# Dealing shared PSUM banks by expected release, moving key transposes and preparation in an attention and MLP kernel

## The chip, the cores and the metric

One core of a Trainium2 chip. TensorE multiplies matrices into eight PSUM banks, VectorE and ScalarE read them and work on SBUF, GpSimd works on SBUF, SyncE starts most DMAs; each engine runs its own list of instructions in order and waits on semaphores. The metric is the device time of one execution in microseconds. Before the change it was 1618.06 us, the median of three (1617.95 to 1619.25).

## The reference

An attention over 8 batches of 8 heads, whose keys and values are means of 8 rows each, and two MLPs one after the other on its 4608 tokens of width 512:

```
k_p = k.reshape(B, H, S // 8, 8, D).mean(axis=3)      # v_p in the same way; S 576, D 64
scores = q @ k_p.T / sqrt(D)
attn = exp(scores - max) / (sum + 1e-9)
x = (attn @ v_p), heads side by side                  # 4608 x 512
h = x @ w_in;   x = max(0.01 h, h) @ w_out            # 512 -> 2048 -> 512
h = x @ w_in2;  out = max(h, 0)**2 @ w_out2
```

## The kernel before

Values are float32 throughout. A large product is made of three matmuls on operands split into a high and a low part (`three`, lines 339 to 341).

The work has stages. The attention runs interleaved with the first three token tiles (512 tokens each) of the first MLP: tile 0 up to about 158 us, tile 1 to 315, tile 2 to 450. A unit of a tile is one block f of 128 hidden columns, 16 to a tile: `first(t, f)` makes `h1_t_f` with 12 matmuls, ScalarE and VectorE turn it into `gh` and `gl`, and `second(t, f)` adds it with 12 matmuls into four accumulators `acc1_t_j`. Between two units `advance()` moves the generator `attention()` on by a few steps. From 450 us on three passes of the first MLP follow ("lead" passes, t 0 to 2), whose products are combined from sums of operands in the manner of Strassen, and five passes of the second MLP. Each pass has two halves, `first2` and `second2`; after each of their steps (a hook) the last loop of the file calls `prepare_step()` as long as fewer steps are done than `PACE * hooks`. Those steps make the operands of the second MLP's weights (`wm`, `ops`, `hl` and `s` tiles on VectorE and ScalarE).

The attention takes each batch in five chunks of queries, at tokens 0, 128, 256 (64 wide), 320 and 448. In tile names a batch and the chunk's token stand behind the kind: `s5_448_0` are the scores of the first four heads of batch 5, chunk 448. For each chunk: `stage_a` transposes the queries (`trq`), `stage_b` makes two banks of scores (`s`), VectorE takes the max (`mx`, L625), then either ScalarE makes eight exponentials out of PSUM (L632, up to batch 5) or VectorE subtracts the max out of PSUM and ScalarE makes one exponential (L637, batches 6 and 7); GpSimd normalizes (`p`, L651, L659); `stage_c` transposes the probabilities (`pt` and the remainder `pr`); `stage_d` makes the outputs `o`.

`prepare_k(b)` prepares the keys of a batch: VectorE adds them pairwise, two halves (L405, L411 into `kd`) and a remainder (`rr`); TensorE transposes them (`trk`, L460, and `trr`, L475); ScalarE copies them into `kT`. For batches 3 to 7 this is put ahead of the last chunk (448) of the batch before.

PSUM has four accumulator banks (`ps_a`) and four shared banks (`ps_w`). Every short-lived tile (`h`, `trq`, `trk`, `trr`, `s`, `pt`, `pr`, `o`) comes from `work()` and takes the next shared bank in turn. A tile that takes a bank waits until the reads of its last user are done. Within these waits a scheduler orders each engine's instructions, so the written order is not quite the built one.

Of the kernel before, what the change touches and what calls it, by code (L numbers as in the profile page):

```python
# [8 lines left out]
F32 = mybir.dt.float32  # L9
# [8 lines left out]
P = 128  # L18
POOL = 8
TT = 512  # L20
# [12 lines left out]
def attention_two_mlps(  # L33
# [24 lines left out]
    EARLY = 6  # L58
# [10 lines left out]
    PADS = {0: 88, 3: 48, SHRUNK: 48}  # L69
    DIFF = 384  # L70
    XSTEPS = 3
    PACE = 0.87
    LEAD = 3
    NPASS = len(HALVES) - LEAD
    HMAX = max(HALVES)
# [23 lines left out]
    ps_w = one_stack.enter_context(tc.tile_pool(name="ps_w", bufs=4, space=PSUM))  # L99
# [45 lines left out]
    def temp(name, dt=F32):  # L145
        return tpool.tile([P, TT], dt, tag="t", name=name)

    def work(name, n=TT, early=False):
        if early:
            return ps_a.tile([P, n], F32, tag="acc", name=name)  # L150
        return ps_w.tile([P, n], F32, tag="w", name=name)

    x0 = [dpool.tile([DM, WIDE[t]], F32, name=f"x0_{t}") for t in range(NTILE)]
    x0 += [dpool.tile([DM, HALVES[i // 2]], F32, name=f"x0_{NTILE + i}") for i in range(2 * LEAD)]
# [189 lines left out]
    def attention():  # L344

        with ExitStack() as s:
# [39 lines left out]
            rr = one.tile([NP * RX, 2, D], F32, name="rr")  # L386
# [15 lines left out]
            def pooled(dst, src):  # L402

                for n in (POOL * D // 2, POOL * D // 4):
                    nc.vector.tensor_tensor(  # L405
                        out=src[:, :, 0:n], in0=src[:, :, 0:n], in1=src[:, :, n:2 * n], op=ALU.add
                    )
                last = [src[:, :, i * D:(i + 1) * D] for i in range(2)]
                if len(dst.shape) == 4:
                    last = [one_of.unsqueeze(2).to_broadcast(list(dst.shape)) for one_of in last]  # L410
                nc.vector.tensor_tensor(out=dst, in0=last[0], in1=last[1], op=ALU.add)  # L411
# [44 lines left out]
            def load_v(b):  # L456
                return load_kv(b, v, "v", nc.scalar if b == 0 else None)

            def turned(tr, kd, m):
                nc.tensor.transpose(tr[:, m * P:(m + 1) * P], kd[:, m].rearrange("p i d -> p (i d)"), ident)  # L460
# [20 lines left out]
            def prepare_k(b):  # L481
                kr, kk = KV.pop(("k", b))
                i = b % 2
                kd = ap1.tile([P, NP, 2, D], F32, tag="kd", name=f"kd{b}")
                if b in K_ON_PE:
                    for ps in pooled_pe(f"kp{b}", kk):
                        yield
                    nc.scalar.copy(kd, ps.unsqueeze(2).to_broadcast([P, NP, 2, D]))
                else:
                    for g in range(2):  # L490
                        pooled(kd[:, 2 * g:2 * g + 2], kk[g])
                        if b > 0:
                            yield
                            continue
                        tr = work("trk0") if g == 0 else tr
                        for m in range(2 * g, 2 * g + 2):
                            turned(tr, kd, m)
                        yield
                pooled(rr[:, 1:2], kr)
                if b > 0:  # L500
                    load_v(b)
                    tr = work(f"trk{b}")
                    for m in range(NP):
                        turned(tr, kd, m)
                put_keys(i, tr, slice(0, NP))
                put_rest(i, b)
                yield
# [63 lines left out]
            for b in range(B):  # L571
                at = 0
                for span in range(len(SPANS)):
                    off = 0
                    while off < SPANS[span]:
                        n = min(P, SPANS[span] - off)
# [22 lines left out]
            pr = {}  # L599
# [128 lines left out]
            nch = len(chunks) // B  # L728
# [160 lines left out]
            def outputs():  # L889
                for b, span in ended:  # L890
                    yield from stage_d(b, span)
                    ready[0] = max(ready[0], b + span)
                ended.clear()

            opened, ended = [nch], []
            for i in range(nch + 1, len(chunks)):
                b = chunks[i][0]
                if i == 2 * nch:
                    while opened:
                        yield from finish(opened.pop(0))  # L900
                        yield from outputs()
                    yield from prepare_k(2)
                if i % nch == nch - 1 and 1 < b < B - 1:
                    yield from prepare_k(b + 1)
                if i + 2 < len(chunks):
                    load_q(*chunks[i + 2])
                if i + 1 < len(chunks):
                    stage_a(*chunks[i + 1])
                    yield
                stage_b(*chunks[i])  # L910
                yield
                opened.append(i)
                yield from outputs()
                if i % nch == LAG[min(b, 2)]:
                    yield from prepare_v(b)
                while len(opened) > LAG[min(b, 2)]:
                    yield from finish(opened.pop(0))
                    if b < 2:
                        yield from outputs()
# [61 lines left out]
            nc.sync.dma_start(out=dst[j * P:(j + 1) * P, at:at + step], in_=o[:, skip:skip + step])  # L981

    def second(t, f):
        gh, gl = G.pop((t, f))
        wh, wl = HL.pop(("out", t, f))
        if f == 0:
            A[t] = [ps_a.tile([P, TT], F32, tag="acc", name=f"acc1_{t}_{j}")[:, :WIDE[t]] for j in range(4)]
        acc = A[t]
        for j in range(4):
            js = slice(j * P, (j + 1) * P)  # L990
            three(acc[j], (wh[:, js], wl[:, js]), (gh, gl), f == 0, f == NF - 1)
        if f == NF - 1:
            for j in range(4):
                o = temp(f"o1_{t}_{j}")[:, :WIDE[t]]
                if j % 2 == 0:
                    nc.scalar.copy(o, acc[j])
                else:
                    nc.vector.tensor_copy(o, acc[j])
                store_x1(t, j, o)
# [11 lines left out]
    FIRST2 = []  # L1011
# [377 lines left out]
    prep, preparing, hooks, prepared = None, True, 0, 0  # L1389
# [34 lines left out]
    for i, (t, f) in enumerate(units):  # L1424
        if f == NF - 3 and t + 1 < NTILE:
            while ready[0] * S < min((t + 2) * TT, PLAIN):
                advance()
            put_stores(made)
            load_x(t + 1)
        if f == NF - 1 and t + 1 < NTILE:  # L1430
            split_x(t + 1)

        rate = RATES[min(t, 1)]
        if i + 1 < len(units):
            first(*units[i + 1])
        tick()
        if i + 2 < len(units):
            split_weights("in", *units[i + 2])
        if i + 1 < len(units):
            split_weights("out", *units[i + 1])  # L1440
        while at_work and made < due + rate // 2:
            advance()
        second(t, f)
        tick()
        due += rate
        while at_work and made < due:
            advance()
        if w1 < NF:
            prepare_weights(w1)
            w1 += 1  # L1450
        elif i >= NF - 2:
            held(lambda: next(sums1, None))
            if i % 4 == 0:
                held(lambda: next(sums1, None))
        if i == NF:
            behind(marks[0], 3000)
        if t == NTILE - 1 and f >= NQ - 2 and not at_work:
            if x2pool is None:
                assert not at_work and next(sums1, 1)
                w_early_stack.close()  # L1460
                x2pool = high_stack.enter_context(tc.tile_pool(name="x2", bufs=1, side="right", reuse_waits="tile"))
                dpart = high_stack.enter_context(tc.tile_pool(name="d2", bufs=1, side="right", reuse_waits="tile"))
                ring = high_stack.enter_context(tc.tile_pool(name="ring", bufs=RING, side="right", reuse_waits="tile"))
                load_x2(0)
                tick(9)
                blocks.insert(0, next_block())
            else:
                if xg is None:
                    xg = products_x(0)
                for _ in range(XSTEPS):  # L1470
                    next(xg, None)
# [23 lines left out]
    for t in range(LEAD + NPASS):  # L1495
        lead[0] = t < LEAD
        if t in (LEAD, SHRUNK):
            assert not preparing
            tick(9)
            pass_stack.close()  # L1500
            low_stack.close()
            if t == SHRUNK:
                xspool.append(ctx.enter_context(tc.tile_pool(name="xs", bufs=1, side="right", reuse_waits="tile")))
            gfpool, gopool, tmpool = open_pools(pass_stack, t)
        for half in (first2, second2):
            for _ in half(t):
                tick()
                hooks += 1
                if prepared < PACE * hooks:
                    prepare_step()  # L1510


# [27 lines left out]
```

## Time and profile before

| | |
|---|---|
| timed runs, median (us) | 1618.06 (1617.95 to 1619.25) |
| profiled execution (us) | 1612.93 |
| its span (us) | 1611.2 |
| TensorE busy (us) | 1574.5, 98% |
| VectorE busy (us) | 1355.0, 84% |
| ScalarE busy (us) | 964.0, 60% |
| GpSimd busy (us) | 120.8, 7% |
| mean granted TensorE clock | 0.997 of 2.4 GHz |

The profile is of one execution; the span reaches from its first to its last instruction. TensorE is PE, VectorE DVE, ScalarE ACT, GpSimd POOL. A busy TensorE may still run slowly or be fed short matmuls; an idle one waits, and the trace says for what.

### The profile page before, as it was taken

The page shows a single profiled execution, that of the slowest core. Times are in us where ns is not written, and L with a number is a line of the kernel's source. Part 1 is how long each engine was busy: PE and PEld are TensorE (multiplying, and loading weights), DVE is VectorE, ACT ScalarE, POOL GpSimd, SP SyncE. Part 2 cuts the span into 40 slices and gives each one's busy share as a digit, 9 for nine tenths or more (in the row PEclk, how much of TensorE's full clock was granted, in tenths as well). Part 3 has the DMA queues.
Part 4 walks back from the last instruction along what each step waited for, and adds up shares of the span by engine and source line. Part 5 has one row for each costly group of instructions (what it writes and reads, how often), then busy time and mean ns, then how long its engine had stood idle before and what let it go on. Part 6 is the DMA issues. An engine that isn't in the chain of part 4 may idle for free.

```text
span 1611.2 us, 23281 instructions
## 1 busy us (share of the span) xinstructions
PE 1574.5 (98%) x7960; PEld 1334.9 (83%) x7960; DVE 1355.0 (84%) x1989; ACT 964.0 (60%) x1827; POOL 120.8 (7%) x146
## 2 busy tenths in 40 slices
PE   6999999999999999999999999999999999999999
PEld 5877787778888887887878888888888888998997
DVE  6999688799588897799779778977897799699797
ACT  6786777755666756675676435643563365465454
POOL 3202332233000000000000000000000000000000
PEclk9999999999999999999999999999999999999999
DMA  8765867663558668867785545454555445656655
GB/s 220 229 199 168 242 198 222 204 188 91 174 201 288 231 200 271 296 205 233 270 308 169 190 141 181 148 183 147 168 174 162 159 141 189 229 170 216 196 165 176
DMA packets 211142, 319.79 MB, mean 198 GB/s; under 512 B 54352, under 2 KB 123984, under 8 KB 211024
## 3 DMA queue, kind: packets, MB, share of 16 engines
q1 hardware_dynamic: 207872, 316.60, 60.7%
q10 hardware_dynamic: 3152, 1.70, 0.4%
q8 instruction: 63, 1.03, 0.3%
q14 instruction: 55, 0.45, 0.1%
HBM read 247.46 MB, written 69.21 MB: 197 GB/s over the span
## 4 chain that ended last, share of the span: by engine, by line
PE 70%; DVE 18%; ACT 4%; DMA 4%; issue 3%; SPq 0%; POOL 0%; ACTq 0%; DVEq 0%; POOLq 0%
PE psum L1255 14%; PE psum L341 13%; PE psum L339 13%; PE psum L340 13%; PE psum L1256 7%; DVE ol L1050 3%; ACT x L632 1%; DVE g L1053 1%; PE h L339 1%; PE s L615 1%; PE h L340 1%; PE h L341 1%; PE acc L339 1%; DVE wb_out L1155 1%; DVE xl L1050 1%
## 5 line engine op out<-in xcount | busy, mean ns | idle before, releaser
L1255 PE MATMUL psum<-wb_out,oh 128*128 128x512 f32 x1008 | 349.7, 392 | 0.0
L339 PE MATMUL psum<-xh,wb_in 128*128 128x512 f32 (+1 forms) x896 | 336.6, 376 | 1.8 <-ACT s L1229 1.0
L341 PE MATMUL psum<-xh,wb_in 128*128 128x512 f32 (+1 forms) x896 | 336.4, 376 | 1.3 <-DVE wb_in L1155 1.3
L340 PE MATMUL psum<-xl,wb_in 128*128 128x512 f32 (+1 forms) x896 | 336.4, 375 | 0.0
L1049 ACT CAST oh<-g 128x1024 fp32r<-128x1024 f32 (+1 forms) x224 | 223.1, 997 | 109.4 <-PE psum L1255 54.0
L1256 PE MATMUL psum<-wb_out,ol 128*128 128x256 f32 x1008 | 281.8, 280 | 0.0
L1050 DVE TENSOR_TENSOR ol<-g,oh 128x1024 fp32r<-128x1024 f32 (+1 forms) x224 | 257.1, 1150 | 8.4 <-ACT oh L1049 7.9
L1255 PEld LDWEIGHTS psum<-wb_out,oh 128*128 128x128 f32 x1008 | 189.2, 188 | 41.8
L339 PEld LDWEIGHTS psum<-xh,wb_in 128*128 128x128 f32 x896 | 168.2, 188 | 29.2 <-ACT s L1229 1.7
L341 PEld LDWEIGHTS psum<-xh,wb_in 128*128 128x128 f32 x896 | 168.2, 188 | 27.9 <-DVE wb_in L1155 1.7
L340 PEld LDWEIGHTS psum<-xl,wb_in 128*128 128x128 f32 x896 | 168.2, 188 | 26.0
L1256 PEld LDWEIGHTS psum<-wb_out,ol 128*128 128x128 f32 x1008 | 189.3, 188 | 0.1
L1154 ACT CAST wb_in<-wb_in 128x512 fp32r<-128x512 f32 x128 | 79.4, 621 | 131.4 <-DMA wb_in<-ws_in 74.6
L1053 DVE TENSOR_TENSOR g<-g,g 128x1024 f32<-128x1024 f32 (+1 forms) x128 | 147.0, 1151 | 0.8 <-ACT g L1176 0.8
L1155 DVE TENSOR_TENSOR wb_in<-wb_in 128x512 fp32r<-128x512 f32 x128 | 87.4, 686 | 61.4 <-ACT wb_in L1154 57.6
L341 PE MATMUL psum<-oh,wb_out 128*128 128x512 f32 x336 | 130.8, 390 | 1.0 <-DVE wb_out L1155 1.0
L340 PE MATMUL psum<-ol,wb_out 128*128 128x512 f32 x336 | 131.3, 391 | 0.0
L339 PE MATMUL psum<-oh,wb_out 128*128 128x512 f32 x336 | 130.7, 389 | 0.0
L1154 ACT CAST wb_out<-wb_out 128x512 fp32r<-128x512 f32 x128 | 79.1, 620 | 53.7 <-DMA wb_out<-ws_out 36.0
L1178 DVE SCALAR_TENSOR_TENSOR g<-g 128x1024 f32<-128x1024 f32 (+1 forms) x80 | 89.1, 1115 | 17.1 <-ACT g L1248 16.4
L1155 DVE TENSOR_TENSOR wb_out<-wb_out 128x512 fp32r<-128x512 f32 x128 | 85.7, 683 | 3.2 <-ACT wb_out L1154 3.1
L339 PE MATMUL h<-xh,hl_in 128*128 128x512 f32 x192 | 78.2, 407 | 4.8 <-ACT hl_out L263 2.1
(171 smaller groups left out, 2781.5 us busy)
## 6 DMA issues: line engine op xcount, KB each, us to landing
wb_in<-wd_in SPq DMA_DIRECT2D x96, 512.0 KB, 3.5
wb_out<-wd_out SPq DMA_DIRECT2D x96, 512.0 KB, 3.9
wb_in<-ws_in SPq DMA_DIRECT2D x128, 256.0 KB, 2.7
wb_out<-ws_out SPq DMA_DIRECT2D x128, 256.0 KB, 2.6
xl<-x SPq DMA_DIRECT2D x24, 512.0 KB, 5.1
v<-in_v_dram SPq DMA_DIRECT2D x16, 512.0 KB, 4.4
st_in_out<-in_moe_w_in_dram SPq DMA_DIRECT2D x16, 512.0 KB, 4.1
st_in_out<-in_moe_w_out_dram SPq DMA_DIRECT2D x16, 512.0 KB, 5.2
```

Of the source, the lines that this page charges most:

```text
L339: nc.tensor.matmul(outp, ah, bh, start=first, stop=False, **kw)
L340: nc.tensor.matmul(outp, ah, bl, start=False, stop=False, **kw)
L341: nc.tensor.matmul(outp, al, bh, start=False, stop=last, **kw)
L615: nc.tensor.matmul(sc[:n, 2 * m:2 * m + 2].rearrange("p a x -> p (a x)"), qT[:, 2 * e + m, :n], kT[b % 2][:, 2 * e + m].rearrange("p a x - ...
L1049: nc.scalar.copy(hi, src)
L1050: nc.vector.tensor_tensor(out=lo, in0=src, in1=raw(hi), op=ALU.subtract)
L1053: nc.vector.tensor_tensor(out=out_, in0=a, in1=b, op=ALU.subtract)
L1154: nc.scalar.copy(whole[:, 0], raw(whole[:, 1]))
L1155: nc.vector.tensor_tensor(out=whole[:, 1], in0=raw(whole[:, 1]), in1=raw(whole[:, 0]), op=ALU.subtract)
L1178: nc.vector.scalar_tensor_tensor(out=g, in0=g, scalar=0.0, in1=g, op0=ALU.max, op1=ALU.mult)
L1255: nc.tensor.matmul(outp, ah, b, start=first, stop=False, skip_group_check=True)
L1256: nc.tensor.matmul(outp[:, 1], al, b[:, 0], start=False, stop=last, skip_group_check=True)
```

## The change

There are three parts. `work()` no longer deals the shared banks in turn from the second tile on: it keeps a clock in units of expected TensorE time (`BUSY`), a time at which each bank is expected to come free (its user's `HOLD` after that user's turn), and gives the bank with the earliest one; `second` moves the clock on by the length of a unit. Keys of batches 3 to 7 have their sums put ahead of the last chunk of the batch before, as until now, but their transposes behind its scores and behind the outputs; the remainder's sum and the loads of the values move up behind the second half's sum. `PACE` becomes a pair: 1.12 steps a hook in the first 28 hooks of a pass, 0.62 in the others.

```
+    HOLD = {"h": 2.2, "trq": 1.6, "trk": 1.8, "trr": 1.5, "pt": 2.2, "pr": 1.8, "o": 1.4}
+    BUSY = {"h": 2.7, "trq": 0.45, "trk": 0.5, "trr": 0.2, "pt": 0.45, "pr": 0.15, "o": 0.5, "s": 0.5}
+    free, clock, chosen = [0.0] * 4, [0.0], [False, 0]
     def work(name, n=TT, early=False):
...
-        return ps_w.tile([P, n], F32, tag="w", name=name)
+        kind = name.split("_")[0].rstrip("0123456789")
+        if chosen[0]:
+            i = min(range(4), key=lambda j: (free[j], (j - chosen[1]) % 4))
+            clock[0] = max(clock[0], free[i]) + BUSY[kind]
+            hold = HOLD.get(kind)
+            if hold is None:
+                b, e = int(name.split("_")[0][1:]), int(name.split("_")[2])
+                hold = (2.4, 2.8)[e] if b >= EARLY else (3.7, 6.0)[e]
+            free[i] = clock[0] + hold
+        else:
+            i = chosen[1]
+        chosen[1] = (i + 1) % 4
+        return ps_w.tile([P, TT], F32, tag=f"w{i}", name=name, bufs=1)[:, :n]
...
                         if b > 0:
+                            if b > 1 and g == 1:
+                                pooled(rr[:, 1:2], kr)
+                                load_v(b)
                             yield
...
                 if i % nch == nch - 1 and 1 < b < B - 1:
-                    yield from prepare_k(b + 1)
+                    keys = prepare_k(b + 1)
+                    for _ in range(2):
+                        next(keys)
+                        yield
...
                 yield from outputs()
+                yield from keys
...
     def second(t, f):
+        clock[0] += BUSY["h"]
...
         rate = RATES[min(t, 1)]
+        chosen[0] = t > 0
...
-    PACE = 0.87
+    PACE = (1.12, 0.62)
...
-                if prepared < PACE * hooks:
+                whole, part = divmod(hooks, 2 * len(FIRST2))
+                more = max(0, part - len(FIRST2))
+                if prepared < sum(PACE) * len(FIRST2) * whole + PACE[0] * (part - more) + PACE[1] * more:
                     prepare_step()
```

On VectorE, before the change, at the hand-over from batch 6 to 7 (`k7_0` and `kd7` are key sums, `pt1_6` and `pt_r` subtractions that read banks of transposed probabilities, `mx6_320` and `x6_320` read score banks):

```order
L405 TENSOR_TENSOR k7_0_4267<-k7_0_4267 128x2x256
L676 TENSOR_TENSOR pt1_6_4276<-pt6_0_4283,pt0_6_4275 128x4x128
L973 TENSOR_TENSOR gl1_2_3_4257<-g1_2_3_4254,gh1_2_3_4256 128x512
L689 TENSOR_TENSOR pt_r_189<-pr6_0_4290,pt_r_189 32x2x128
L405 TENSOR_TENSOR k7_0_4267<-k7_0_4267 128x2x128
L288 TENSOR_TENSOR s1_in6_4238<-s1_in6_4238,w1_6_827 128x256
L411 TENSOR_TENSOR kd7_4351<-k7_0_4267 128x256
L289 TENSOR_TENSOR s1_in6_4238<-w1_6_827,s1_in6_4238 128x256
L264 TENSOR_TENSOR hl_in_2_5_4376<-w1_5_743,hl_in_2_5_4376 128x512
L625 TENSOR_REDUCE mx6_320_0_4325<-s6_320_0_4319 128x4
L625 TENSOR_REDUCE mx6_320_1_4327<-s6_320_1_4322 128x4
L637 TENSOR_TENSOR x6_320_4316<-s6_320_0_4319,mx6_320_0_4325 128x288
```

And of the changed kernel at the same place (its lines are numbered 16 to 25 higher there):

```order
L697 TENSOR_TENSOR pt1_6_4276<-pt6_0_4283,pt0_6_4275 128x4x128
L998 TENSOR_TENSOR gl1_2_3_4257<-g1_2_3_4254,gh1_2_3_4256 128x512
L304 TENSOR_TENSOR s1_in6_4238<-s1_in6_4238,w1_6_827 128x256
L710 TENSOR_TENSOR pt_r_189<-pr6_0_4290,pt_r_189 32x2x128
L305 TENSOR_TENSOR s1_in6_4238<-w1_6_827,s1_in6_4238 128x256
L280 TENSOR_TENSOR hl_in_2_5_4376<-w1_5_743,hl_in_2_5_4376 128x512
L421 TENSOR_TENSOR k7_0_4267<-k7_0_4267 128x2x256
L646 TENSOR_REDUCE mx6_320_0_4325<-s6_320_0_4319 128x4
L646 TENSOR_REDUCE mx6_320_1_4327<-s6_320_1_4322 128x4
L658 TENSOR_TENSOR x6_320_4316<-s6_320_0_4319,mx6_320_0_4325 128x288
```

The first key sum moved behind six operations, and the other two of that half behind the score subtractions.

On TensorE, before, at the hand-over from batch 5 to 6 (`trk6` transposes keys, `s5_448` are the last chunk's scores):

```order
L686 MATMUL pr5_128_3791<-ident_149,p5_128_3506 96x128 x2
L339 MATMUL acc1_1_0_1959<-gh1_1_15_3722,hl_out_1_15_3732 128x512
L340 MATMUL acc1_1_0_1959<-gl1_1_15_3723,hl_out_1_15_3732 128x512
L460 MATMUL trk6_3815<-ident_149,kd6_3796 128x128 x2
L341 MATMUL acc1_1_0_1959<-gh1_1_15_3722,hl_out_1_15_3732 128x512
L339 MATMUL acc1_1_1_1960<-gh1_1_15_3722,hl_out_1_15_3732 128x512
```

And of the changed kernel there:

```order
L707 MATMUL pr5_128_3791<-ident_149,p5_128_3506 96x128 x2
L636 MATMUL s5_448_0_3827<-kT1_181,qT5_448_3742 128x144 x2
L476 MATMUL trk6_3897<-ident_149,kd6_3796 128x128 x2
L355 MATMUL acc1_1_0_1959<-gh1_1_15_3722,hl_out_1_15_3732 128x512
L356 MATMUL acc1_1_0_1959<-gl1_1_15_3723,hl_out_1_15_3732 128x512
L357 MATMUL acc1_1_0_1959<-gh1_1_15_3722,hl_out_1_15_3732 128x512
```

Two acc matmuls moved behind the first keys, and the scores of chunk 448, which stood behind the first `h` of the next tile, stand ahead of the keys.

On TensorE, before, in batch 3, from the scores of chunk 320 on:

```order
L615 MATMUL s3_320_1_2619<-kT1_181,qT3_320_2401 128x144 x2
L671 MATMUL pt3_128_2640<-ident_149,p3_128_2378 128x128 x4
L686 MATMUL pr3_128_2647<-ident_149,p3_128_2378 96x128 x2
L339 MATMUL acc1_1_0_1959<-gh1_1_6_2566,hl_out_1_6_2576 128x512
L340 MATMUL acc1_1_0_1959<-gl1_1_6_2567,hl_out_1_6_2576 128x512
L341 MATMUL acc1_1_0_1959<-gh1_1_6_2566,hl_out_1_6_2576 128x512
L339 MATMUL acc1_1_1_1960<-gh1_1_6_2566,hl_out_1_6_2576 128x512
L340 MATMUL acc1_1_1_1960<-gl1_1_6_2567,hl_out_1_6_2576 128x512
L341 MATMUL acc1_1_1_1960<-gh1_1_6_2566,hl_out_1_6_2576 128x512
L339 MATMUL h1_1_7_2661<-xh1_1_0_1773,hl_in_1_7_2573 128x512
```

And of the changed kernel there:

```order
L636 MATMUL s3_320_1_2619<-kT1_181,qT3_320_2401 128x144 x2
L692 MATMUL pt3_128_2640<-ident_149,p3_128_2378 128x128 x4
L707 MATMUL pr3_128_2647<-ident_149,p3_128_2378 96x128 x2
L355 MATMUL acc1_1_0_1959<-gh1_1_6_2566,hl_out_1_6_2576 128x512
L356 MATMUL acc1_1_0_1959<-gl1_1_6_2567,hl_out_1_6_2576 128x512
L357 MATMUL acc1_1_0_1959<-gh1_1_6_2566,hl_out_1_6_2576 128x512
L355 MATMUL acc1_1_1_1960<-gh1_1_6_2566,hl_out_1_6_2576 128x512
L636 MATMUL s3_448_0_2713<-kT1_181,qT3_448_2598 128x144 x2
L356 MATMUL acc1_1_1_1960<-gl1_1_6_2567,hl_out_1_6_2576 128x512
```

After the chunk's transposed probabilities there were six acc matmuls and then an `h`; now there are four, and then the scores of the last chunk.

## Rows read from the trace of the kernel before

**Rows 1.** First part of the page: busy time of each engine, share, instructions.

```profile
PE 1574.5 (98%) x7960; PEld 1334.9 (83%) x7960; DVE 1355.0 (84%) x1989; ACT 964.0 (60%) x1827; POOL 120.8 (7%) x146
```

**Rows 2.** Stretches: length, then busy time (instructions) by engine, granted clock, DMA.

```profile
50.00:100.00 50.00, 47.86 (x249) 39.80 (x248) 49.05 (x76) 38.33 (x87) 10.40 (x9) 0.97 0.67 210
150.00:300.00 150.00, 146.24 (x811) 119.66 (x810) 115.80 (x252) 115.90 (x452) 47.58 (x59) 1.00 0.71 217
300.00:450.00 150.00, 142.24 (x757) 116.28 (x755) 122.92 (x260) 90.01 (x212) 38.12 (x43) 1.00 0.51 154
450.40:526.60 76.20, 76.20 (x336) 63.12 (x337) 63.09 (x88) 50.39 (x67) 0.00 (x0) 1.00 0.78 269
526.60:603.40 76.80, 76.80 (x338) 62.84 (x337) 72.09 (x100) 50.27 (x73) 0.00 (x0) 1.00 0.63 208
```

**Rows 3.** TensorE's waits from 450 to 920: us in total, times, longest.

```profile
PE psum L341 <- DVE wb_in L1155: 1.3, 1, 1.3
PE psum L339 <- ACT s L1229: 1.0, 1, 1.0
PE psum L341 <- DVE wb_out L1155: 1.0, 1, 1.0
```

**Rows 4.** VectorE's timeline at 348: start, length, operation, [idle before, releaser].

```profile
348.25 1.82 DVE L405 TENSOR_TENSOR k<-k 128x512 f32<-128x512 f32 x1 [1.71 <-DMA k<-in_k_dram]
...
354.55 0.81 DVE L637 TENSOR_TENSOR x<-s,mx 128x288 f32<-128x288 f32 x2
```

**Rows 5.** TensorE's timeline, 351 to 361.

```profile
351.86 0.63 PE L671 MATMUL pt<-ident,p 128*128 128x128 f32 x4 [0.38 <-DVE pt_r L689]
...
355.14 0.47 PE L339 MATMUL h<-xh,hl_in 128*128 128x512 f32 x1 [1.74 <-DVE x L637]
...
360.75 0.44 PE L460 MATMUL trk<-ident,kd 128*128 128x128 f32 x2 [0.79 <-DVE kd L411]
```

**Rows 6.** TensorE's timeline, 85 to 88.

```profile
85.92 0.47 PE L339 MATMUL h<-xh,hl_in 128*128 128x512 f32 x1 [2.14 <-ACT hl_out L263]
...
86.47 0.39 PE L341 MATMUL h<-xh,hl_in 128*128 128x512 f32 x1
86.69 0.40 PE L339 MATMUL h<-xh,hl_in 128*128 128x512 f32 x1
...
87.54 0.63 PE L339 MATMUL h<-xh,hl_in 128*128 128x512 f32 x1
87.97 0.63 PE L340 MATMUL h<-xl,hl_in 128*128 128x512 f32 x1
```

**Rows 7.** TensorE's timeline, 310 to 323.

```profile
310.37 0.41 PE L460 MATMUL trk<-ident,kd 128*128 128x128 f32 x2 [1.50 <-DVE rs L645]
...
314.26 0.24 PE L475 MATMUL trr<-ident,rr 64*128 64x64 f32 x1 [0.90 <-DVE rr L411]
...
322.84 0.50 PE L339 MATMUL acc<-gh,hl_out 128*128 128x512 f32 x1 [1.39 <-ACT o L996]
```

**Rows 8.** VectorE's timeline, 307 to 311.

```profile
307.86 1.96 DVE L405 TENSOR_TENSOR k<-k 128x512 f32<-128x512 f32 x4
...
310.26 0.64 DVE L676 TENSOR_TENSOR pt<-pt,pt 128x512 fp32r<-128x512 f32 x1
```

**Rows 9.** TensorE's waits from 100 to 450: us in total, times, longest.

```profile
PE o L339 <- ACT x L632: 1.4, 3, 0.5
...
PE pt L671 <- POOL p L651: 1.2, 1, 1.2
PE s L615 <- ACT x L632: 1.0, 2, 0.5
```

**Rows 10.** TensorE's timeline, 220 to 225.

```profile
220.51 1.14 PE L615 MATMUL s<-kT,qT 128*128 128x144 f32 x8
...
224.41 0.51 PE L339 MATMUL h<-xh,hl_in 128*128 128x512 f32 x1 [0.71 <-ACT x L632]
```

**Rows 11.** VectorE's timeline at 607, ahead of the operand `wb_in`.

```profile
606.67 0.68 DVE L245 CUSTOM_DVE_ANT_0 ops_out<-ops_out,wm_out 128x1024 uint16<-128x1024 uint16 x1
```

More of the change, by code (lines that the diff above doesn't have):

```diff
@@ L498, in prepare_k @@
                         yield
-                pooled(rr[:, 1:2], kr)
+                if b < 2:
+                    pooled(rr[:, 1:2], kr)
+                if b == 1:
+                    load_v(b)
                 if b > 0:
-                    load_v(b)
                     tr = work(f"trk{b}")
@@ L893, in outputs @@
                 ended.clear()
-            opened, ended = [nch], []
+            opened, ended, keys = [nch], [], iter(())
             for i in range(nch + 1, len(chunks)):
```

## The prediction

> **What bounds the kernel now.** I read the page's busy times first, then busy time by stretch, then TensorE's waits, then the timelines around the longest of them. TensorE is busy 98% of a span of 1611.2 us [rows 1], so a change of order can only give back idle time, and where that lies decides everything. By stretch [rows 2] TensorE is idle 3.8 us in 150 to 300 us (150 less 146.24) and 7.8 us in 300 to 450 (150 less 142.24). In the first Strassen-like pass of layer 1, from 450.4 on, both half passes show TensorE busy throughout. The new dealing of banks starts with the second tile, at about 158 us, and the new order of the keys a little later, so those two parts have 3.8 + 7.8 = 11.6 us to win at most. The preparation by half passes has the waits of the three lead passes, 1.3 + 1.0 + 1.0 = 3.3 us [rows 3].
>
> **Keys of the last batch (hand-over from batch 6 to 7).** Here the trace shows a cause and its effect. VectorE stands 1.71 us at 348.25 before `k<-k`, the first key sum, because the DMA of the keys has not landed, and then spends 1.82 us in it [rows 4]. The sums of the probabilities, the max of the scores and their subtraction stand behind it. TensorE therefore waits .38 at 351.86 for a bank (pt_r), 1.74 at 355.14 for the subtraction at 354.55 that frees a score bank, and .79 at 360.75 for the second half of the key means [rows 4, 5]. A matmul that restarts the engine is .08 longer than its neighbours (0.47 at 85.92 against 0.39 at 86.47) [rows 6], so these are 2.91 + 3 x .08, about 3.2 us. In the built order the first key sum stands behind six operations that it delayed before, and the second one behind the score subtraction of chunk 320; both transposes of the keys now stand after eight acc matmuls. The DMA has landed by 348.25 [rows 4]; the sum's new place comes after that, so VectorE doesn't stop. The sum still stands ahead of the max: 1.82 us instead of 1.71 + 1.82, and the six operations that pass it now fill the stop, so scores are subtracted about 1.7 us earlier (354.55 less 1.71), as much as the wait of 1.74. The transposes come 2 us of acc matmuls later, which covers the .79. I take -3.2. Bounds: -3.2 (nothing is left) and -.5 (only the pt_r wait of .38 and its restart go).
>
> **Keys of batch 6 (hand-over from 5 to 6).** TensorE waits 1.50 at 310.37 for the first key means, .90 at 314.26 for the rest keys, 1.39 at 322.84 for an accumulator that ScalarE copies out behind eight exponentials [rows 7]: 3.79 + 3 x .08 = 4.0. Now the scores of chunk 448 stand ahead of the transposes, and wait for the bank that the probabilities' subtraction frees. That subtraction (310.26) ran behind the four key sums (1.96 from 307.86) [rows 8]; it now stands ahead, so it ends between 308.9 (310.26 - 1.96 + .64) and 309.5, as its ScalarE half may lie between exponentials. TensorE comes there two acc matmuls earlier than to the old wait: 310.37 - 1.50 - 2 x .23 = 308.4. So a new wait of .5 to 1.1; I take 1.1. The later key sums keep a wait of about .7 of the .90, and the accumulator's wait about half of its 1.39, since those exponentials start earlier. Left: 1.1 + .7 + .7 = 2.5, a gain of 1.5. Bounds: -4.0 (all goes) and +1.0 (the new wait is added and only the transposes' 1.50 shrinks by half).
>
> **Banks dealt by expected release, batches 2 to 5.** The waits there name the exponentials: .71 for `h`, 1.4 for `o`, 1.0 for `s` [rows 9, 10]. A score bank is held from 220.51 until the exponentials have read it at 224.41, 3.9 us [rows 10], while TensorE comes back for it 3.2 us later (3.9 - .71). Any dealing must wait for such a bank if all four are held. In the new order of batch 3, scores `s3_448_0` take the place of `h1_1_7` behind the bank of `s3_320_0`, with four acc matmuls between instead of six; two matmuls of .23 fewer make the wait .46 longer. Batch 4 shows the same shift by .43 at its hand-over. Against that, I let .4 of the `o` and `s` waits go, where an output gets a bank that a transpose held. Sum +.46 + .43 - .4, about +.5. Bounds: -3.1 (all three kinds go) and +4.4 (the wait of 1.17, which is .71 + .46, at four more places is 4.7, less .3 regained).
>
> **First tile.** It deals in turn still, but the values of batch 2 load a step earlier, and their sums on VectorE and their mask on GpSimd now stand ahead of the last probabilities of batch 1, for which TensorE waits 1.2 [rows 9]. Between -1.2 (it goes) and +1.2 (it doubles); two h matmuls (.46) now stand ahead of that wait, and some .8 of vector sums too: +.3.
>
> **Preparation by half passes.** The pace rises by .25 a hook in the first 28 hooks and falls by .25 in the others: 7 steps a pass moved forward, on paper. VectorE is busy 63.09 of 76.20 us in a first half and 72.09 of 76.80 in a second [rows 2]; seven steps of the 1.2 us that the largest takes would fit into the first half (71.5). But the order built from it has nearly as many preparation instructions per half as before (42, 15, 42, 18, 44, 7 against 42, 14, 42, 18, 41, 11 on VectorE): the queues were already ahead of the pace. Of the three waits [rows 3] the one for `wb_in` has one `ops_out` instruction more ahead of it (pitch .6) [rows 11] and the others the same work. Take +.3; bounds -3.3 (all three go) and +1.2 (two such steps). What hides the rest of these moves is the second half's slack of 4.7 us; if it were gone, each moved step would cost its 1.2.
>
> **Sum.** -3.2 - 1.5 + .5 + .3 + .3 = -3.6 us. Against the profiled execution: it took 1612.93, the span 1611.2 and 1.7 around it; 1609.3 after. That run lies 5.13 us below the median of the timed ones, 1618.06, and I put the same difference on it: 1614.5 us.
>
> **TensorE's clock.** After the wait of 2.14 us at 85.92 the h matmuls of 87.54 and later start .43 apart, against .22 at 86.47, and the granted clock of 50 to 100 is .97 [rows 2, 6]: the engine fell to the lower of its two levels, 1.2 GHz for 2.4. After the 1.74 us at 355.14 [rows 5] the granted clock of the stretch stays at 1.00 [rows 2]. So a longer wait can be paid a second time, twelve matmuls x .20 = 2.4 us, as it was paid there from 87.5 to 90.1. The Trainium skill, "TensorE: Matmul & The Clock Gate", section "Part 1: The HAM clock gate (the "warmup" mystery)", says that the throttled clock is the default and activity releases it. By that rule, new waits of the change could cost more than they last; the trace agrees at 85.92 and shows no fall after the wait at 355.14. It speaks against a change that puts scores ahead of other work at a full set of banks. The sum would be 1614.5 without and 1616.9 with one such fall.
>
> **Rivals.**
> A. The waits only move: whoever comes next at a held bank waits as long. For: the releases are set by ScalarE's exponentials and VectorE's chain, and neither gets shorter; TensorE arrives earlier wherever a wait was removed. Against: the stop at 348.25 is a stop for a DMA, and it goes. The time is then 1618 (1616 to 1620).
> B. The dealing works as its table says. Of the 11.6 us, all but about 1.5 go: 10 us less, 1608. For: four banks in turn make a free bank wait behind a held one. Against: [rows 10] show a hold of 3.9 us, which exceeds the work at hand whoever gets the bank.
> C. Slower: at the five hand-overs the scores of the last chunk are put ahead of the key transposes and reach a bank still under the previous chunk's exponentials. Price: 3.9 us of hold less the work between, 1.17 us each, 5 x 1.17 = 5.9, less the .71 that it replaces: +5.2, 1623, if the two late hand-overs gain nothing besides. It decides as soon as the hold exceeds the four acc matmuls and two transposes between. For: the hold of 3.9 us [rows 10]. Against: in batches 6 and 7 the scores are freed by one subtraction, not by four exponentials. If the clock falls once as at 85.92, it is 1625.6; that has .03 of its chance.
> D. The change doesn't do what it says: the pace moves nothing, as counted above. That alone costs nothing and is in the forecast.
>
> **How the numbers follow.** Forecast (1611 to 1616) .42; A .26; B .16; C .16. A measurement of this kernel tells about .2%, 3.2 us, from no change. So faster means below 1614.8, same 1614.8 to 1621.3. The forecast's case is split, .34 faster and .08 same; A is all same; B all faster; C slower, but for .01 that ends under the bound. Faster .50, same .35, slower .15. The likeliest case's own range is 1611 to 1616; for 8 in 10 I reach to B's 1608 and, as A is likelier than C, to 1620.5: 1607.5 to 1620.5. The bounds summed, -14.8 to +7.3 from 1618.06, are wider, but their ends need every term to fall the same way.
>
> **What would show it.** Around 348 VectorE no longer stops before `k<-k`, and the wait of 1.74 at the h matmul that follows is under .5: right for the first term. A wait of `s` for a bank at the hand-over to batch 6 of about 1.1, and together under 2.5 there, for the second. Waits of `s3_448_0` and `s4_448_0` of 1.2 for the third. If TensorE's idle time from 150 to 300 falls below 2 us, B was right; if it rises above 7, C. The lead passes should keep three waits of about 1 us. It is wrong if idle time from 300 to 450 stays near 7.8, or if a new stop with a lower granted clock appears.

## The result, and the profile after

The changed kernel takes 1624.57 us, the median of five (1623.49 to 1626.43), against 1617.95 for the kernel before, timed with it (five runs, 1613.13 to 1619.25). The ratio is 1.0058, 95% interval 1.0041 to 1.0074: slower by 0.4 to 0.7%, where 1614.5 and faster was forecast, and above the range's upper end of 1620.5. The two medians alone differ by 6.6 us, the lower end of that interval, since the five runs of before fall into two groups, three at 1618 to 1619 and two at 1613. The profiled execution took 1625.12 us, its span 1623.4; that is 12.2 us above the profiled span of before.

First part of the page of after, which answers to [rows 1]:

```profile
PE 1581.7 (97%) x7960; PEld 1337.3 (82%) x7960; DVE 1361.2 (84%) x1989; ACT 967.5 (60%) x1827; POOL 118.2 (7%) x146
```

TensorE is busy 7.2 us longer with as many instructions. So more than half of the difference between the two profiles is no idle time at all. Where it lies shows when stretches are cut at the same matmuls in both traces, not at the same times. Here are first `h` of tile 0 to first `h` of tile 1, from there to the last `h` of tile 2, and from there to the end of the lead passes, before and then after (columns as in [rows 2]):

```profile
39.43:158.26 118.83, 114.31 (x568) 93.59 (x569) 114.59 (x183) 90.73 (x201) 20.80 (x15) 0.99 0.61 195
158.26:441.21 282.95, 271.90 (x1488) 222.53 (x1487) 223.09 (x481) 195.25 (x641) 84.89 (x100) 1.00 0.63 191
441.21:915.27 474.06, 469.93 (x2066) 386.58 (x2064) 414.57 (x573) 310.53 (x418) 0.00 (x0) 1.00 0.71 239
```

```profile
42.10:163.22 121.12, 115.20 (x571) 93.29 (x570) 114.96 (x184) 91.53 (x201) 20.25 (x15) 0.99 0.64 196
163.22:450.80 287.58, 274.86 (x1489) 222.47 (x1488) 228.07 (x479) 196.08 (x641) 82.74 (x100) 1.00 0.61 186
450.80:927.32 476.52, 471.23 (x2065) 386.68 (x2064) 415.23 (x573) 312.06 (x418) 0.00 (x0) 1.00 0.72 237
```

| stretch | before | after | more |
|---|---|---|---|
| up to the first h | 39.43 | 42.10 | 2.67 |
| first tile | 118.83 | 121.12 | 2.29 |
| second and third tile | 282.95 | 287.58 | 4.63 |
| lead passes | 474.06 | 476.52 | 2.46 |
| all that follows | | | 0.1 |

The first 2.67 us are not the change's: below, executions of kernels alike up to there reach that matmul at 39.4 to 39.7 us or at 42.1 to 42.7. In the second and third tile the busy time alone grows by 2.96 (274.86 less 271.90) and the idle time by 1.67. So waits make the smaller part of the loss there.

**The waits that answer to the forecast.** VectorE of after at the last key hand-over, for [rows 4]:

```profile
354.30 0.82 DVE L579 SCALAR_TENSOR_TENSOR vM<-vd,side_of,vM 128x256 fp32r<-128x256 f32 x2
356.45 0.69 DVE L697 TENSOR_TENSOR pt<-pt,pt 128x512 fp32r<-128x512 f32 x1 [1.33 <-ACT pt L694]
...
360.58 0.69 DVE L421 TENSOR_TENSOR k<-k 128x512 f32<-128x512 f32 x1
...
362.04 0.81 DVE L658 TENSOR_TENSOR x<-s,mx 128x288 f32<-128x288 f32 x2
```

ScalarE at the same place:

```profile
355.34 0.60 ACT L994 ACTIVATE g<-h 128x512 f32<-128x512 f32 x1 [1.58 <-PE h L357]
355.84 0.58 ACT L694 CAST pt<-pt 128x512 fp32r<-128x512 f32 x1
```

and TensorE, for the wait of 1.74 in [rows 5]:

```profile
362.63 0.47 PE L355 MATMUL h<-xh,hl_in 128*128 128x512 f32 x1 [1.09 <-DVE x L658]
```

The stop for the DMA is gone, as forecast; in its place VectorE stops 1.33 us before the subtraction `pt`, for ScalarE's cast `pt`, which stands behind an activation of `h` that ends 355.94. Part of that second stop had been hidden behind the first: before, VectorE stood still from 346.54 (348.25 less 1.71), and the same cast ended only at 347.43.

```profile
346.85 0.58 ACT L673 CAST pt<-pt 128x512 fp32r<-128x512 f32 x1
```

The `h` matmul still waits 1.09. At the hand-over to batch 6 the six waits of TensorE in the trace of after, the two of the scores (.64 and .27) among them, sum to 3.2 us; the forecast had 2.5.

TensorE in batch 3, for [rows 10]:

```profile
225.05 1.22 PE L636 MATMUL s<-kT,qT 128*128 128x144 f32 x8
...
227.46 0.40 PE L355 MATMUL acc<-gh,hl_out 128*128 128x512 f32 x1
230.20 0.76 PE L636 MATMUL s<-kT,qT 128*128 128x144 f32 x4 [2.35 <-ACT x L653]
230.70 0.49 PE L356 MATMUL acc<-gl,hl_out 128*128 128x512 f32 x1
231.03 0.39 PE L357 MATMUL acc<-gh,hl_out 128*128 128x512 f32 x1
231.26 0.40 PE L355 MATMUL acc<-gh,hl_out 128*128 128x512 f32 x1
```

The scores of chunk 448 reach the bank of the scores before them and wait 2.35 us; [rows 10] had .71 at that bank for an `h`. The bank is held 5.2 us (225.05 to 230.20) and not 3.9, because the max comes late from VectorE and the exponentials begin 3.8 us after the first of those scores, before 2.5:

```profile
228.83 0.32 ACT L653 ACTIVATE x<-s,mx 128x72 f32<-128x72 f32 x1 [2.96 <-DVE mx L646]
```

Mark 230.70 to 231.03 too: after a change of operands the second matmul starts .33 behind the first, the next ones .23. TensorE of after changes between kinds of tile some 290 times in the second and third tile, before 262 times, and 29 x .1 would make the 2.96 us of busy time. But the number of changes alone does not make it. The dealing alone has 317 changes and as much more busy time (274.93), and the four tags in turn have 280 and no more busy time than before (271.39):

```profile
161.05:447.76 286.71, 274.93 (x1488) 222.18 (x1487) 224.94 (x478) 195.37 (x641) 85.56 (x100) 1.00 0.62 186
164.26:446.10 281.84, 271.39 (x1489) 222.89 (x1487) 222.51 (x478) 194.65 (x641) 84.15 (x100) 1.00 0.63 189
```

What makes the busy time longer stays open.

TensorE's waits of after in the lead passes, for [rows 3]:

```profile
PE psum L356 <- DVE ol L1076: 1.7, 2, 0.9
PE psum L355 <- ACT s L1255: 1.3, 1, 1.3
PE psum L355 <- ACT oh L1075: 1.2, 1, 1.2
```

Waits for conversions of the pass, `ol` twice and `oh`, stand where two for weights (`wb`) were.

### The profile page after: what moved, and what is told of

It reads as the page before. It is cut to its first block, busy times and chain, and to the rows that moved or that the text cites. A ratio compares the mean times of both kernels' runs of the same rounds, so it can differ in the third digit from the quotient of the medians.

```text
span 1623.4 us, 23240 instructions
## 1 busy us (share of the span) xinstructions
PE 1581.7 (97%) x7960; PEld 1337.3 (82%) x7960; DVE 1361.2 (84%) x1989; ACT 967.5 (60%) x1827; POOL 118.2 (7%) x146
## 4 chain that ended last, share of the span: by engine, by line
PE 70%; DVE 17%; ACT 4%; issue 4%; DMA 3%; POOL 0%; SPq 0%; ACTq 0%; DVEq 0%; POOLq 0%
PE psum L1281 14%; PE psum L356 13%; PE psum L357 13%; PE psum L355 13%; PE psum L1282 7%; DVE ol L1076 2%; ACT x L653 2%; PE h L355 1%; PE h L356 1%; PE h L357 1%; DVE g L1079 1%; PE s L636 1%; DVE mx L646 1%; PE acc L355 1%; PE acc L356 1%
```

## The experiments

Each ratio is to the kernel before on the same chip, with its 95% interval; in the experiments the median of before was 1614.9 to 1615.4. The third column is the ratio's excess times 1615.

| kernel | ratio | more, us | tiles on a bank not the first free |
|---|---|---|---|
| before | 1 | | 3 of 236 |
| after | 1.0058 [1.0041, 1.0074] | 9.4 | 95 of 241 |
| dealing alone | 1.0055 [1.0043, 1.0067] | 8.9 | 95 of 239 |
| keys alone | 1.0004 [0.9996, 1.0013] | 0.6 | 6 of 238 |
| pace alone | 1.0018 [1.0008, 1.0029] | 2.9 | |
| four tags, in turn | 1.0006 [0.9997, 1.0014] | 1.0 | 40 of 241 |
| dealing, measured table | 1.0038 [1.0024, 1.0051] | 6.1 | 51 of 241 |
| keys and pace | 1.0021 [1.0011, 1.0030] | 3.4 | 6 of 239 |
| keys all late | 1.0015 [1.0006, 1.0024] | 2.4 | 7 of 239 |
| pace turned round | 1.0000 [0.9991, 1.0009] | 0.0 | |
| banks as the pool gave them | 1.0015 [1.0005, 1.0026] | 2.4 | 17 of 239 |
| dealing from tile 2 on | 1.0027 [1.0015, 1.0038] | 4.4 | 46 of 241 |

The last column is read from one trace each: of the tiles that take a shared bank between 158 and 455 us, those whose bank's last read ended over .3 us later than that of another bank at that point of the dealing (good to about 2). The count does not set the price by itself: the four tags in turn have 40 such tiles and cost 1.0, the banks as the pool gave them 17 and 2.4.

**The dealing alone.** The edits to `work()`, `second` and `chosen` of the change, the rest as before.

```
...
-        return ps_w.tile([P, n], F32, tag="w", name=name)
+        return ps_w.tile([P, TT], F32, tag=f"w{i}", name=name, bufs=1)[:, :n]
...
```

> Only the dealing of the shared banks (with its four one-bank tags); keys and pace as before. Theory 1 (the dealing costs): 5 to 7 us slower than before, about 2 of it in the first tile (40 to 158 us), the rest between 158 and 315. Theory 2 (the key order costs): within 2 us of before. Theory 3 (the extra 12 us of the two profiled runs is mostly the start-up): within 2 us, and any difference lies before 45 us.

1624.02 us, 1.0055: theory 1. The dealing is nearly all of the loss.

**Keys alone.** The edits to `prepare_k` and the loop over chunks.

```
-                    yield from prepare_k(b + 1)
+                    keys = prepare_k(b + 1)
...
```

> Only the keys' transposes behind the scores, banks in turn and pace as before. Theory 1: 1 to 3 us faster, since the stop of VectorE before the keys of batch 7 goes and the first tile is not touched. Theory 2: 4 to 6 us slower, with new waits of the last chunks' scores at the five hand-overs, 1.2 us each.

1616.16 us, 1.0004: neither; the gain is not there, nor is the loss. TensorE at the hand-over to batch 6 in this kernel:

```profile
319.76 0.27 PE L475 MATMUL trr<-ident,rr 64*128 64x64 f32 x1 [1.46 <-ACT x L637]
321.02 0.43 PE L676 MATMUL pt<-ident,p 64*128 64x64 f32 x4 [0.98 <-issue]
...
323.76 0.80 PE L339 MATMUL acc<-gh,hl_out 128*128 128x512 f32 x1 [1.93 <-ACT o L1005]
...
326.20 0.63 PE L341 MATMUL acc<-gh,hl_out 128*128 128x512 f32 x1
326.62 0.63 PE L339 MATMUL acc<-gh,hl_out 128*128 128x512 f32 x1
```

Three waits of 1.46, .98 and 1.93 us follow within 6 us, and up to 328.33 the matmuls start some .43 apart; the granted clock of this stretch is .77:

```profile
315.00:330.00 15.00, 10.53 (x42) 8.14 (x41) 11.41 (x26) 6.85 (x28) 5.71 (x5) 0.77 0.69 210
```

New waits took the old ones' place, and the lower of the clock's two levels cost some 10 x .20 more. And VectorE's first key sum stands where it stood, with its stop:

```profile
352.72 0.80 DVE L405 TENSOR_TENSOR k<-k 128x512 f32<-128x512 f32 x1 [1.37 <-DMA k<-in_k_dram]
```

**Pace alone.**

```
-    PACE = 0.87
+    PACE = (1.12, 0.62)
...
```

> Only the pace of the preparation, 1.12 and 0.62 a hook instead of 0.87. Theory 1: 1.5 to 3 us slower, all of it in the lead passes (450 to 915 us): the waits of oh and ol operands that the changed kernel shows at 545, 613 and 755 come from it. Theory 2, as predicted: within 0.5 us, the three waits of about 1 us stay and no new one comes.

1617.55 us, 1.0018: theory 1, and its profile is 3.1 us longer in the lead passes. SyncE's queue of this kernel in the second pass, and what follows on ScalarE and TensorE:

```profile
720.54 0.33 SPq L215 DMA_DIRECT2D st_out_out<-in_moe_w_out_dram  x1
...
721.40 0.42 SPq L215 DMA_DIRECT2D st_out_out<-in_moe_w_out_dram  x1
722.51 3.04 SPq L1143 DMA_DIRECT2D wb_out<-ws_out  x2
```

```profile
729.67 0.62 ACT L1154 CAST wb_out<-wb_out 128x512 fp32r<-128x512 f32 x1 [3.55 <-DMA wb_out<-ws_out]
730.19 1.04 ACT L1049 CAST oh<-g 128x1024 fp32r<-128x1024 f32 x1
```

```profile
731.29 0.50 PE L339 MATMUL psum<-oh,wb_out 128*128 128x512 f32 x1 [0.65 <-ACT oh L1049]
732.55 0.50 PE L340 MATMUL psum<-ol,wb_out 128*128 128x512 f32 x1 [0.76 <-DVE ol L1050]
```

Before, SyncE issued these two loads of `st_out_out` nearly 11 us later:

```profile
731.29 0.33 SPq L215 DMA_DIRECT2D st_out_out<-in_moe_w_out_dram  x1
...
732.15 0.42 SPq L215 DMA_DIRECT2D st_out_out<-in_moe_w_out_dram  x1
```

Moved forward, they stand ahead of the weights `wb_out` on their queue. ScalarE stops 3.55 us for those weights with the conversion `oh` queued behind, and TensorE waits for `oh` and for `ol`, .65 and .76. This is one place; in the whole of its lead passes the waits for `oh` and `ol` sum to 4.2 us, where before had 3.3 for weights and `s`. The term was counted on VectorE and ScalarE, where little moves; the loads that a step issues were left out.

**Four tags, in turn.** The dealing alone with `chosen` never set:

```
-        chosen[0] = t > 0
+        chosen[0] = False
```

> The four shared banks as four tags of one bank each, but dealt strictly in turn throughout; keys and pace as before. If the way in which the banks are declared, not the choice among them, moves the first tile: 1.5 to 3 us slower than before, the difference made between 40 and 158 us, and the dealing kernel adds 3 to 4 to it. If the choice alone costs: within 0.5 us of before.

1615.86 us, 1.0006: the choice costs, some 8 us of the 9. But the first tile is 2.8 us longer in the trace, as in every kernel with the four tags (2.3 to 3.4), and the same wait is new there; TensorE's waits of after and of this kernel in the first tile:

```profile
PE h L355 <- ACT g L994: 1.6, 1, 1.6
```

```profile
PE h L355 <- ACT g L985: 1.8, 1, 1.8
```

In its profile the second and third tile give 1.1 of that back. And with the keys in their old order VectorE's first key sum of batch 7 stands behind the subtraction `pt` here, without a stop for the DMA:

```profile
357.74 0.69 DVE L421 TENSOR_TENSOR k<-k 128x512 f32<-128x512 f32 x1
```

So the four tags move that sum, not the new order of the keys.

**The table mended.** The dealing alone with holds from the trace of before.

```
-    HOLD = {"h": 2.2, "trq": 1.6, "trk": 1.8, "trr": 1.5, "pt": 2.2, "pr": 1.8, "o": 1.4}
+    HOLD = {"h": 0.9, "trq": 1.0, "trk": 1.75, "trr": 0.9, "pt": 2.1, "pr": 2.75, "o": 1.65}
...
-                hold = (2.4, 2.8)[e] if b >= EARLY else (3.7, 6.0)[e]
+                hold = (2.45, 2.35)[e] if b >= EARLY else (2.75, 2.95)[e]
```

> The dealing alone (keys and pace as before), with its table set to the holds that the trace of before shows (first write to last read, less BUSY: h 0.9, trq 1.0, trk 1.75, trr 0.9, pt 2.1, pr 2.75, o 1.65, scores 2.75 and 2.95, in the last two batches 2.45 and 2.35). Theory A, the table is wrong: at most 2 us slower than before, as the four tags in turn, and under 40 of some 240 tiles get a bank that is not the first to come free. Theory B, a bank fixed in written order cannot follow the order that is built: still 5 us or more slower, 60 or more of such tiles.

1621.63 us, 1.0038. Closer to theory B, with the count of wrong banks between the two: from 95 to 51. The second score bank of a chunk was down with 6.0 us and its median in batches 2 to 5 is 3.8 from first write to last read. The better table gives back some 3 us (the intervals overlap a little), not 8.

**Keys and pace.** The change without the dealing.

> The changed kernel with the pool's own dealing of the shared banks: keys and pace changed. Theory A and B alike (the dealing costs 8 us, the pace 3, the keys nothing): 2 to 5 us slower than before. If the parts cost by working together instead: within 1 us of before, or 7 us and more slower.

1617.86 us, 1.0021, as the sum of the parts, 0.6 + 2.9. With the dealing's 8.9 the parts sum to 12.4, above the 9.4 (6.6 to 12.0) of the whole; so the parts may not be quite independent.

**Keys all late.** The whole preparation behind the scores and outputs.

```
-                if i % nch == nch - 1 and 1 < b < B - 1:
-                    yield from prepare_k(b + 1)
...
                 yield from outputs()
+                if i % nch == nch - 1 and 1 < b < B - 1:
+                    yield from prepare_k(b + 1)
```

> Banks and pace as before; the whole preparation of the keys of batches 3 to 7, sums as well as transposes, written behind the last chunk's scores and the outputs. If VectorE's stop before the first key sum causes the wait of 1.74 us at the h matmul of 355, as predicted: the stop and that wait go, and the time is 1 to 3 us below before, unless the later transposes delay the next batch. If another chain sets that wait: no change there, and the time within 1 us, or 2 to 4 us slower where the first scores of the next batch wait for the keys.

1616.95 us, 1.0015, slower. VectorE's stop for the DMA goes, and the wait at that `h` with it, but a stop of 1.23 us for ScalarE's `pt` appears, and TensorE waits 1.10 for the keys and .74 for a subtraction of scores:

```profile
352.97 0.69 DVE L676 TENSOR_TENSOR pt<-pt,pt 128x512 fp32r<-128x512 f32 x1 [1.23 <-ACT pt L673]
```

```profile
365.80 0.44 PE L460 MATMUL trk<-ident,kd 128*128 128x128 f32 x2 [1.10 <-DVE kd L411]
...
367.85 0.43 PE L671 MATMUL pt<-ident,p 64*128 64x64 f32 x4 [0.74 <-DVE x L637]
```

**Pace turned round.**

```
-    PACE = 0.87
+    PACE = (0.62, 1.12)
...
```

> Only the pace, turned round: 0.62 steps a hook in the first half of a pass and 1.12 in the second. If steps moved forward cost because their loads and ScalarE conversions come in front of operands of the pass: 1 to 3 us faster than before, with fewer waits in the lead passes. If any move away from an even pace costs: 2 to 5 us slower, with new waits in the second halves, where VectorE is busy 72 of 77 us already.

1615.03 us, 1.0000: neither. In time, held-back steps cost nothing and win nothing. But its profiled execution was the slowest of its eleven, and its lead passes there take 477.5 us, 3.4 more than before's and as long as with the pace of the change (477.1). So the traces do not show where the 2.9 us of that pace lie.

**Banks as the pool gave them.** The four tags, with the kernel before's own bank for each tile name.

```
+        if name in AS_BUILT:
+            i = AS_BUILT[name]
...
```

> The four one-bank tags, each tile by its name in the very bank that the pool gave it in the kernel before; keys and pace as before. If the choice of the bank is what costs: within 2 us of before, and about as many tiles as there (3 of 236) get a bank that is not the first to come free. If a bank fixed at the time of writing costs by itself, whichever it is: 5 us or more slower, with the first tile 2 to 3 us longer.

1618.05 us, 1.0015: between the two, nearer to the first. The first tile is again 3.1 us longer; second and third tile take 281.3 us, no more than before. A list of banks does not bring the order back: 22 of the 321 shared tiles are still first written behind one that the code takes later.

**Dealing from the third tile on.**

```
-        chosen[0] = t > 0
+        chosen[0] = t > 1
```

> The dealing by expected release from the third tile on only (t over 1) instead of the second, in turn before; keys and pace as before. If it costs wherever it deals: between the four tags in turn (+0.9) and the dealing alone (+9), about 4 to 6 us slower, the second tile (158 to 315 us) as long as with the tags in turn. If the second tile's four exponential-bound batches make the cost: under 2 us slower.

1618.93 us, 1.0027: it costs wherever it deals, about half (4.4 of 8.9) with one tile instead of two. Of these runs none beats the kernel before.

## Why the prediction was wrong

**The step that failed is the term on the banks, +.5 us, and with it what is said above of the kernel before: that it deals its banks in turn.** It does not. The first shared tiles of before lie on banks 0 3 2 1 3 0 2 1 0 2 3 1 2 0 3 2, and later all but 3 of 236 lie on one that came free first. Its shared tiles are first written in the very order in which the code takes them, and the pool of one tag gives each a bank that is free at that point of the built order. The change fixes the bank where a tile is written in the code, before the times are known, and with four tags the order itself comes apart as well: in turn 32 of the 321 shared tiles are first written behind one that the code takes later, in the changed kernel 51, in the kernel before none. I read "in turn" off the source. So rival B's premise was false, and the term was priced as a few waits that lengthen. One place shows what a bank fixed beforehand costs: at 403.31 an `h` of after waits for a bank whose last reader is VectorE's `pt`, while the bank of `trq` had been read at 401.37.

```profile
403.31 0.50 PE L355 MATMUL h<-xh,hl_in 128*128 128x512 f32 x1 [1.79 <-DVE pt L697]
```

```profile
402.57 0.68 DVE L697 TENSOR_TENSOR pt<-pt,pt 128x512 fp32r<-128x512 f32 x1
```

```profile
400.78 0.59 ACT L618 COPY qT<-trq 128x512 f32<-128x512 f32 x1
```

The term measured 8.9 us with the first tile's part, 2.3 to 3.4 in the traces, where the forecast had .3, and that for other work, because the dealing is in turn there. TensorE there in after and in before:

```profile
133.90 0.50 PE L355 MATMUL h<-xh,hl_in 128*128 128x512 f32 x1 [1.58 <-ACT g L994]
...
135.71 0.66 PE L692 MATMUL pt<-ident,p 128*128 128x128 f32 x4 [1.08 <-POOL p L672]
```

```profile
129.98 0.66 PE L671 MATMUL pt<-ident,p 128*128 128x128 f32 x4 [1.19 <-POOL p L651]
130.39 0.48 PE L339 MATMUL h<-xh,hl_in 128*128 128x512 f32 x1
```

The `h` has passed the `pt` that stood before it, and waits for the activation that frees its bank; the `pt` behind it still waits. With the banks as the pool gave them this `h` has the same bank as in the kernel before and waits 1.6 us all the same. So here the changed order costs, not the wrong bank.

The choice adds the rest, some 8 us by the runs. By what mechanism is shown only in part: in the dealing's own trace the second and third tile are 3.8 us longer, .7 of it idle and 3.0 busy time, whose cause is open.

**The keys, -3.2 and -1.5, measured +0.6.** The new place of VectorE's key sum, on which the first term rested, is not the keys' doing: in the keys' own kernel, and in keys and pace, the stop for the DMA stays (1.37 and 1.53 us), and with four tags and the old keys it goes. I read it off the changed kernel as a whole and put it down to the wrong part. And waits that were to go had others right behind them: the DMA's stop one for ScalarE's cast, and the accumulator's wait stayed in the keys' own trace (1.93; in after's .26, where an `h` waits .81 instead). A wait names only who came last; I took it as all there was.

**The pace, +.3, measured +2.9.** The loads on SyncE's queue were not counted, and at one place they make TensorE wait 1.4 us; that they make the whole is not shown.

**The base and the clock.** The 1618.06 us from which the forecast starts were three runs; the experiments put before at about 1615. A clock fall was priced at twelve matmuls x .20, but from 87.54 to 90.10 there are six.

**What held.** Rival C named the mechanism of the longest new wait, that of `s3_448_0`. That its time, 1623, is near is luck: the scores of chunk 448 wait 2.35 and .64 at two hand-overs instead of 1.17 at five, the rest of the loss is not its, and in the keys' own kernel `s3_448_0` does not wait at all. The clock's second payment is shown, in the keys' kernel. By the marks set: idle time from 300 to 450 stayed at 7.8 (150 less 142.2), which was to show the forecast wrong; from 150 to 300 it is 5.0, neither B's nor C's.

What stays open besides the busy time: with an even pace the lead passes are 2.4 to 2.9 us longer in the traces of the dealing, the four tags and the banks as given, and 1.8 shorter with the mended table. No run tells why; it is as much as the pace's whole price.

## What to carry to other kernels

Before improving on an allocator, look at what it does in the built program: count from the trace how often it gives a buffer that is not the first to come free. No choice made where the code is written beat the pool's own here, not even the list of the pool's own banks, since splitting one tag into four also sets the order of the tiles free. Ask of each effect in the built program which part of the change makes it, by building the parts alone. A wait that goes is worth no more than the distance to the next one behind it, and a step moved forward takes its loads past other loads.

## What was not expected of the hardware

Executions begin in two ways. TensorE's granted clock from 34 to 42 us was 1.00 in one and .57 in the other, and the first `h` starts at 39.4 to 39.7 us in the first and at 42.1 to 42.7 in the second. The kernel with the pace turned round, which is the kernel before up to the lead passes, is of the second kind (.57, and 42.53 against 39.43). Before and after here, one of each:

```profile
34.00:42.00 8.00, 6.89 (x35) 5.15 (x35) 7.01 (x12) 5.25 (x15) 0.58 (x1) 1.00 0.49 150
```

```profile
34.00:42.00 8.00, 7.18 (x29) 6.03 (x30) 5.93 (x12) 4.42 (x13) 1.50 (x2) 0.57 0.44 140
```

So one profile each can differ by 3 us without a cause in the kernel, which is as much as the smallest parts here. And the longest wait alone does not tell of a clock fall: in the keys' kernel the clock fell with three waits of 1 to 2 us within 6 us (granted clock .77), while the one of 2.35 at 230.20 left matmuls .23 apart.
